# Projections and token sums as two 64-row products side by side, with PSUM in two-bank tiles

## The chip, the cores and the metric

The kernel runs on one core of one Trainium2 chip. Its time is the device time of one execution in microseconds (us); the figure to be predicted is the median of the runs of the changed kernel.

## What is computed

The reference runs four residual blocks over 2048 tokens of width 512, A, B, A, B, each on a layer norm of x. H = 32 heads of 16 columns.

```python
def _A_ref(x, wq, wk, wv, wo, beta):          # segments of 512 tokens, four of them
    ...
    for s in range(N):
        logits = jnp.einsum('bhqd,bhkd->bhqk', qs, ks) * scale + mask
        p = _softmax(logits, axis=-1)
        a_dot = jnp.einsum('bhqk,bhkd->bhqd', p, vs)
        pq = phi(qs)
        num = jnp.einsum('bhld,bhde->bhle', pq, M)
        den = jnp.einsum('bhld,bhd->bhl', pq, z)[..., None] + 1e-06
        o = g * (num / den) + (1.0 - g) * a_dot
        pk = phi(ks)
        M = M + jnp.einsum('bhld,bhle->bhde', pk, vs)
        z = z + jnp.einsum('bhld->bhd', pk)
    return o @ wo

def _B_ref(x, wqkv, w_phi, wo):
    ...
    phi_q = jnp.concatenate([_softmax(pq, axis=-1), _softmax(-pq, axis=-1)], axis=-1)
    phi_k = jnp.concatenate([_softmax(pk, axis=-1), _softmax(-pk, axis=-1)], axis=-1)
    kv = jnp.einsum('bhsf,bhsd->bhfd', phi_k, v)
    z = jnp.einsum('bhsf->bhf', phi_k)
    o = num / den                              # as above, with phi_q, kv and z
    return o @ wo

x = x + _A_ref(_layernorm(x), ...); x = x + _B_ref(_layernorm(x), ...)   # twice
```

The mask of A lets a query see the keys up to and including itself, inside its segment. All tensors are bf16; sums are kept in f32.

## The kernel before

x stays in SBUF as 16 tiles of 128 tokens (`X`). Everything is written as operations in a graph (`Graph.op`), each with the tiles it reads and writes. The order of all operations and the buffer of every tile are not decided when the kernel is built: they come from a table, `ORDER`, that was worked out beforehand and is unpacked in `Graph.place`. `Graph.emit` then walks through that order and puts a semaphore wait ahead of an operation wherever a dependency on another engine is not yet covered. Two operations of PE need none between them, since PE works in program order.

The stages, for each of the two layers:

- `ln` makes the layer norm of a token tile and transposes it into `xT`, mostly by a DMA transpose (`tr`), sometimes on PE through PSUM (`tpe`).
- `a_proj` makes, for one segment of four token tiles and each of four groups g of eight heads, K and Q with the group's columns on the partitions (`wproj`), and V with tokens on the partitions. Each is a sum over four blocks of 128 input columns, so four products of 128 rows and 512 columns into one PSUM bank. K and Q are copied to SBUF (`Kev`, `Qev`); K is also spread into masked copies (`Km`), and `phi` makes the feature maps. The segment's memory sums (`M`) are products over tokens, 136 columns wide.
- `a_att` makes, for a query tile i and each group, the transposed scores in 64-row products: half of the array works on heads from partitions 0 to 63, the other half on those from 64 to 127, and each writes a PSUM bank of its own. ACT takes the exponential, and the products with V (34 columns, 64 rows) accumulate over the keys in two banks `PV`. `a_mem` adds the memory's part. `out_proj` transposes the tile's output and multiplies it by the output weights, four products of 512 columns; the residual is added from PSUM, either by DVE or, where `RES_PE` says so, by a fifth product with the identity.
- `b_keys` makes K and V of block B per token tile (`vproj`), the exponentials, and the token sums (`KV`), 136 columns for each of eight slots, three slots to a bank, added up by `kv_add`.
- `b_query` makes Q of block B (`wproj`, two groups into one two-bank tile), exponentials, the denominators (`Zq`), the products with the sums (`N`) and the output projection.

A product of 64 rows names its half of the array by a tile position; in this text, products of 128 rows and products of 64 rows are two modes of the array. Scores, the products with V, `NM` and `N` have 64 rows, all other products have 128.

PSUM has eight banks. The kernel holds them in two pools:

```python
dbl = [self.es.enter_context(nc.psum_tensor(f"D{i}", [128, 1024], F32)) for i in range(2)]
sgl = [self.es.enter_context(nc.psum_tensor(f"G{i}", [128, 512], F32)) for i in range(4)]
```

`pD`, two tiles of two banks, takes scores, `N`, `NM` and the queries of B. `pG`, four tiles of one bank, takes the projections, transposes and sums (class `gen`), the accumulators (`pv`, two at a time) and the denominators (`nz`). In the profile they appear as D and G.

Of the kernel before, what the change touches and what calls it, by code (L numbers as in the profile page):

```python
# [16 lines left out]
D = 512  # L17
H = 32
# [65 lines left out]
class Op:  # L84
    __slots__ = ("id", "ch", "deps", "succ", "tiles", "opens", "nd", "prio", "eng", "start", "end", "kind", "lat",
                 "label", "seq", "idx", "need", "waits", "tick", "sem", "ndma", "vc", "__dict__")
# [3 lines left out]
class Graph:  # L90
# [39 lines left out]
    def op(self, ch, reads=(), writes=(), opens=(), kind="c", lat=None, label="", ndma=0, port=False, kb=0, rows=128):  # L130
        o = Op()
        o.id = len(self.ops)
        o.ch = ch
        o.deps = set()
        o.succ = []
        o.tiles = []
        o.opens = list(opens)
        o.kind = kind
        o.lat = lat
        o.label = label  # L140
        o.ndma = ndma
        o.need = False
        o.port = port
        o.kb = kb
        o.rows = rows
        o.vc = None
        for r in reads:
            self._touch(o, r, False)
        for w in writes:
            self._touch(o, w, True)  # L150
        o.deps.discard(o)
        self.ops.append(o)
        return o
# [35 lines left out]
    def emit(self):  # L189
# [25 lines left out]
        for o in order:  # L215
# [17 lines left out]
            cand = [d for d in deps if not (d.kind == "c" and d.eng == "pe" and e == "pe") and not covers(kn, d)]  # L233
# [63 lines left out]
class Kernel:  # L297
# [30 lines left out]

    def act(self, out_ap, in_ap, func, n, reads, writes, opens=(), scale=1.0, psum=True, label=""):
        dur = n / 1.2 + (51 if psum else 93)  # L330
        return self.g.op({"act": (dur, lambda e: e.activation(out_ap(), in_ap(), func, scale=scale))},  # L331
                         reads, writes, opens, label=label)
# [18 lines left out]
    def tpe(self, out_ap, src, reads, writes, opens=(), label="", ev=None):  # L351

        ps = self.T(self.pG, "gen")
# [22 lines left out]
    def alloc(self):  # L376
# [44 lines left out]
        dbl = [self.es.enter_context(nc.psum_tensor(f"D{i}", [128, 1024], F32)) for i in range(2)]  # L421
        sgl = [self.es.enter_context(nc.psum_tensor(f"G{i}", [128, 512], F32)) for i in range(4)]
        self.pD = Pool("pD", dbl, psum=True)
        self.pG = Pool("pG", sgl, psum=True)
        self.pG.caps = CAPG
        self.pG.fifo = ("pv",)
        self.pools = [self.pK, self.pX, self.pQ, self.pV, self.pW, self.pE, self.p1, self.p2, self.pT, self.pS, self.pD, self.pG]
# [94 lines left out]
    def fold_weights(self):  # L522
# [12 lines left out]
        for k in ("k", "q"):  # L535
# [7 lines left out]
            for dt in range(4):  # L543
                ps = self.T(self.pG, "gen")
# [40 lines left out]
    def wproj(self, ps, col, W, wres, g, xT, opens=(), label=""):  # L585
        self.mm(lambda: [(ps.t[:, col:col + 512], W[:, dt, g * 128:(g + 1) * 128], xT.t[:, dt, :], dt == 0, dt == 3) for dt in range(4)],
                [512] * 4, [xT[i] for i in range(4)] + wres, [ps[col]], opens=opens, label=label)

    def vproj(self, ps, W, wres, tt, xT, opens=(), label=""):
        self.mm(lambda: [(ps.t[:, 0:512], xT.t[:, dt, tt * 128:(tt + 1) * 128], W[:, dt, :], dt == 0, dt == 3) for dt in range(4)],  # L590
                [512] * 4, [xT[tt]] + wres, [ps[0]], opens=opens, label=label)

    def phi(self, ps, dst, src=None):
# [3 lines left out]
        self.act(lambda: e_.t[:], lambda: ps.t[:, 0:512], ACT.Exp, 512, [ps[0]], [e_], label="phexp")  # L597
        if src is None:
            self.g.op({"dve": (602, lambda e: e.tensor_scalar(dst.t[:], ps.t[:, 0:512], 0.0, None, op0=ALU.max)),
                       "act": (478, lambda e: e.activation(dst.t[:], ps.t[:, 0:512], ACT.Relu))}, [ps[0]], [dst], label="phmax")  # L600
        else:
            v(lambda e: e.tensor_scalar(dst.t[:], src.t[:], 0.0, None, op0=ALU.max), 202, [src], [dst], label="phmax", port=True)
# [23 lines left out]
    def a_proj(self, L, s):  # L626
# [7 lines left out]
        for g in range(NG):  # L634
            ps = self.T(self.pG, "gen")
# [3 lines left out]
            KM = self.T(self.pQ, "KM")  # L639
            pk = self.T(self.p1, "phiKT") if s < 3 else None  # L640
            self.wproj(ps, 0, self.WA["k"], [R("WA", "k", g // 2)], g, xT, opens=[KT] + ([pk] if pk else []), label="K")
# [16 lines left out]
            ps = self.T(self.pG, "gen")  # L658
            QT = self.T(self.pK, "QT")
            PQ = self.T(self.p1, "phiQ") if s >= 1 else None  # L660
            self.wproj(ps, 0, self.WA["q"], [R("WA", "q", g // 2)], g, xT, opens=[QT] + ([PQ] if PQ else []), label="Q")
            self.evac(lambda QT=QT: QT.t[:], lambda ps=ps: ps.t[:, 0:512], 512, [ps[0]], [QT], label="Qev")
            st["QT"].append(QT)
            if PQ:
                self.phi(ps, PQ, QT)
                st["PhQ"].append(PQ)
        for tt in range(4):
            ps = self.T(self.pG, "gen")
            self.mm(lambda tt=tt, ps=ps: [(ps.t[:, 0:512], xT.t[:, dt, tt * 128:(tt + 1) * 128],
                                           self.WA["v"][:, dt, :].rearrange("p (k a e) -> p a k e", k=8, a=2), dt == 0, dt == 3) for dt in range(4)],  # L670
                    [512] * 4, [xT[tt]] + [R("WAv", i) for i in range(4)], [ps[0]], opens=[VT], label="V")
            self.evac(lambda tt=tt: VT.t[:, tt, :, 0:16], lambda ps=ps: ps.t[:, 0:512].rearrange("p (h d) -> p h d", h=H),
                      512, [ps[0]], [VT[tt]], label="Vev")
# [7 lines left out]
        if s < 3:  # L681
            for hp in range(2):
                ps = self.T(self.pG, "gen")
                gs = (hp * 2, hp * 2 + 1)
                self.mm(lambda gs=gs, ps=ps: [
                    (ps.t[:, (g % 2) * 136:(g % 2 + 1) * 136].rearrange("p (k a e) -> p a k e", k=2, a=2), st["PhK"][g].t[:, tt * 128:(tt + 1) * 128],
                     VT.t[:, tt].rearrange("p (a k r) c -> p a k (r c)", a=2, r=2)[:, :, 2 * g:2 * g + 2, :], tt == 0, tt == 3) for g in gs for tt in range(4)],
                        [136] * 8, [st["PhK"][g] for g in gs] + [VT[i] for i in range(4)], [ps[0]], label="M")
                pv = lambda ps=ps: ps.t[:, 0:272].rearrange("p (g h c) -> p g h c", g=2, h=8)
# [8 lines left out]

    def pvitem(self, PV, c, P, V, st, sp):

        a = PV.t[:, c:c + 17]
# [4 lines left out]
    def a_mem(self, L, s, i):  # L706
# [5 lines left out]
        if i == 0:  # L712
            st["mem"] = []
            Rm = st["rm"] = self.T(self.pS, "Rm")
            mc = self.T(self.pG, "nz")
            col = lambda q, g: mc.t[:, (q // 2) * 64:(q // 2) * 64 + 64].rearrange("p (a t g h) -> p a t g h", a=2, t=2, g=NG)[:, :, q % 2, g, :]
            self.mm(lambda: [(col(q, g), PQ[g].t[:, q * 128:(q + 1) * 128], self.MSb[mb][:, g, :, 16], True, True)
                             for q in range(4) for g in range(NG)], [8] * 16, list(PQ) + ms, [mc], opens=[Rm], label="NMd")
            self.g.op({"act": (158.0, lambda e: e.activation(Rm.t[:, 0:128], mc.t[:, 0:128], ACT.Ln, bias=self.eps6[:, 0:1]))},
# [12 lines left out]
    def a_att(self, L, s, i):  # L732
# [11 lines left out]
        PV = [self.T(self.pG, "pv") for _ in range(2)]  # L744
        for g in range(NG):
# [36 lines left out]
            def pvmm(PTs=PTs, g=g, hfs=(0, 1)):  # L782
                r = []
                for hf in hfs:
                    for p in range(2):
                        k = 4 * g + 2 * hf + p
                        for j in range(i + 1):
                            for x in range(2):
                                for ab in range(2):
# [6 lines left out]
                                    r.append(self.pvitem(PV[ab], 18 * k, P, V, j == 0 and x == 0, j == i and x == 1))  # L796
                return r
            vs = [VS[(z, hf)] for z in range(i * VSP // 4 + 1) for hf in range(2)]
            for hfs in ((0,), (1,)) if i in SPLIT else ((0, 1),):
                self.mm(lambda pvmm=pvmm, hfs=hfs: pvmm(hfs=hfs), [], PTs + [PTs[i][0], PTs[i][1]] + [VT[j] for j in range(i + 1)] + vs,  # L800
                        [PV[0][(g, hfs[0])], PV[1][(g, hfs[0])]], label="PV", rows=64, dur=4 * len(hfs) * (i + 1) * 25.5)
        for ab in range(2):
            pvv = lambda ab=ab: PV[ab].t[:, 0:288].rearrange("p (h c) -> p h c", c=18)
            rd = lambda ab=ab: rden().rearrange("p (k a r) -> p k a r", a=2, r=2)[:, :, ab, :]
            v(lambda e, pvv=pvv, rd=rd: self.recip(e, rd(), pvv()[:, :, 16].rearrange("p (k r) -> p k r", r=2)), self.dur_recip(16),
              [PV[ab][(g, h)] for g in range(NG) for h in (range(2) if i in SPLIT else range(1))], [Rt[ab]], label="rden")
# [3 lines left out]
              [PV[ab][(g, h)] for g in range(NG) for h in (range(2) if i in SPLIT else range(1))] + [Rt[ab]], [o[ab]], label="pvn")  # L810
# [5 lines left out]
        self.out_proj(t, o, [o[0], o[1]], self.WA["o"], [R("WA", "o")], pe=("a", L, t) in PE_T)  # L816

    def out_proj(self, t, o, ores, W, wres, store=False, res_pe=False, pe=False, pair=None):
        R = self.R
        oT = self.T(self.p1, "oT")  # L820
        if pair is not None:
            tp = self.T(self.pG, "gen")
# [9 lines left out]
        elif pe:  # L832
# [3 lines left out]
        ps = self.T(self.pG, "gen")  # L836
        if res_pe:
            self.mm(lambda: [(ps.t[:, 0:512], self.ident[:], self.X[:, t, :], True, False)] +
                    [(ps.t[:, 0:512], oT.t[:, dt * 128:(dt + 1) * 128], W[:, dt, :], False, dt == 3) for dt in range(4)],
                    [512] * 5, [oT, R("X", t), R("ident")] + wres, [ps[0]], label="Wo")  # L840
            self.evac(lambda: self.X[:, t, :], lambda: ps.t[:, 0:512], 512, [ps[0]], [R("X", t)], label="res")
        else:
            self.mm(lambda: [(ps.t[:, 0:512], oT.t[:, dt * 128:(dt + 1) * 128], W[:, dt, :], dt == 0, dt == 3) for dt in range(4)],
                    [512] * 4, [oT] + wres, [ps[0]], label="Wo")
# [322 lines left out]
```

## Time and profile before

| | before |
|---|---|
| median of 3 runs | 508.94 us (506.62 to 509.52) |
| the profiled execution | 507.85 us, of which the span of the profile is 506.1 |
| PE matmul | 461.6 us busy (91%), 10514 recorded |
| PE weight load | 291.1 us (58%), 10610 |
| DVE | 437.6 us (86%), 1088 instructions |
| ACT | 439.1 us (87%), 612 |
| granted PE clock, mean over the span | 0.99 |
| DMA | 30.25 MB, 60 GB/s on the mean |

The profile is one execution, recorded by the hardware. "Busy" is the time in which an engine had an instruction under way; matmuls overlap in the array, so a matmul's own duration (380 ns for 512 columns) is longer than the time between the starts of two of them. A row such as `D<-pK,pQ 64*128 64x128` is a product into a tile of the pool D, with 64 rows, 128 output partitions and 128 columns. Some matmul records are missing from the trace; all weight loads are there.

### The profile page before, as it was taken

The numbers are of one execution on the slowest core, as the hardware profiler recorded it, in microseconds if no ns is written. First come the engines' busy times: TensorE is split into PE (matmuls) and PEld (weight loads), VectorE is DVE, ScalarE is ACT, GpSimd is POOL, SyncE is SP. The second block draws the span as 40 slices with busy tenths as digits, with TensorE's granted clock in tenths as the row PEclk, the third lists the DMA queues.
The fourth block names the chain that finished last, engine by engine and source line by source line (L and its number), as shares of the span: only waits on it lengthen the run. The fifth ranks groups of instructions, "written<-read, shape, count | busy, mean of one in ns | idle before, by whom it ended". The sixth has DMA issues, their size and how long they took to land.

```text
span 506.1 us, 23397 instructions
## 1 busy us (share of the span) xinstructions
PE 461.6 (91%) x10514; PEld 291.1 (58%) x10610; DVE 437.6 (86%) x1088; ACT 439.1 (87%) x612; POOL 60.1 (12%) x144
## 2 busy tenths in 40 slices
PE   8899899999888979999999898988998898899896
PEld 4356656555666666555545665566566656565543
DVE  5999969998887978989999888988988788899795
ACT  3899899999899979589999899998998898858993
POOL 3602201100010011101310120110001101010000
PEclk9999989999999999999999999999999999999799
DMA  8943744321213031000235636221221313200165
GB/s 240 230 103 65 105 63 72 42 59 30 52 31 54 4 49 30 12 3 12 33 70 80 76 67 76 54 50 21 55 46 25 45 24 49 31 13 0 37 123 157
DMA packets 89444, 30.25 MB, mean 60 GB/s; under 512 B 76000, under 2 KB 89344, under 8 KB 89344
## 3 DMA queue, kind: packets, MB, share of 16 engines
q1 hardware_dynamic: 88992, 28.46, 30.8%
q8 instruction: 83, 1.36, 1.1%
q10 hardware_dynamic: 288, 0.26, 0.2%
q14 instruction: 17, 0.14, 0.1%
q0 software_dynamic: 64, 0.02, 0.1%
HBM read 6.32 MB, written 2.10 MB: 17 GB/s over the span
## 4 chain that ended last, share of the span: by engine, by line
PE 64%; ACT 13%; DVE 11%; issue 6%; DMA 3%; POOL 2%; POOLq 0%
PE G L325 42%; PE D L325 21%; ACT p L331 9%; ACT pE L331 2%; DVE pQ L644 2%; DMA p<-p 2%; DVE stats L554 2%; DMA beta_sb<-in_A_beta_dram 1%; DVE X L845 1%; POOL rstd L564 1%; PE G L827 1%; DVE p L575 1%; ACT pS L331 1%; DVE p L340 0%; DVE p L985 0%
## 5 line engine op out<-in xcount | busy, mean ns | idle before, releaser
L331 ACT ACTIVATE p<-D 128x1024 bf16<-128x1024 f32 x256 | 256.4, 1039 | 16.2 <-PE D L325 14.9
L325 PE MATMUL D<-pK,pQ 64*128 64x128 bf16 (+1 forms) x2560 | 114.1, 212 | 7.1 <-issue 2.7
L331 ACT ACTIVATE pE<-D 128x768 bf16<-128x768 f32 x128 | 103.0, 828 | 18.7 <-PE D L325 18.2
L325 PEld LDWEIGHTS D<-pK,pQ 64*128 64x128 bf16 x2560 | 71.6, 94 | 60.0 <-issue 20.1
L325 PE MATMUL G<-pV,p 64*128 64x34 bf16 (+1 forms) x1632 | 79.4, 178 | 5.0 <-issue 4.3
L331 ACT ACTIVATE p<-G 128x512 bf16<-128x512 f32 x112 | 67.9, 624 | 13.7 <-PE G L325 11.8
L325 PEld LDWEIGHTS G<-pV,p 64*128 64x128 bf16 (+1 forms) x1632 | 71.4, 93 | 10.0 <-issue 5.8
L325 PE MATMUL G<-pW,pE 64*128 64x34 bf16 x1024 | 71.6, 175 | 5.5 <-issue 5.5
L325 PE MATMUL G<-pV,pE 64*128 64x34 bf16 x1024 | 73.9, 175 | 0.5 <-issue 0.5
L325 PE MATMUL G<-pW,p 64*128 64x34 bf16 x1536 | 70.7, 176 | 1.8 <-issue 1.8
L325 PEld LDWEIGHTS G<-pW,p 64*128 64x128 bf16 x1536 | 64.6, 93 | 2.5 <-issue 2.0
L562 POOL TENSOR_SCALAR rstd<-mv 128x1 f32<-128x1 f32 x60 | 15.6, 265 | 382.9 <-DVE mv L555 382.8
L325 PEld LDWEIGHTS G<-pV,pE 64*128 64x128 bf16 x1024 | 53.4, 93 | 2.5 <-issue 2.4
L325 PEld LDWEIGHTS G<-pW,pE 64*128 64x128 bf16 x1024 | 50.9, 92 | 6.1 <-issue 6.1
L644 DVE TENSOR_SCALAR pQ<-p,m 128x512 bf16<-128x512 bf16 x128 | 43.9, 364 | 0.2
L554 DVE BATCH_NORM_STATS2 stats<-X 128x6 f32<-128x512 bf16 x64 | 43.1, 684 | 0.8 <-DMA X<-in_A_x_dram 0.2
L906 DVE TENSOR_REDUCE pS<-p 128x32 f32<-128x512 bf16 x64 | 42.0, 671 | 1.4 <-ACT p L331 1.4
L845 DVE TENSOR_TENSOR X<-X,G 128x512 bf16<-128x512 bf16 x48 | 32.6, 682 | 10.6 <-PE G L325 10.3
L888 DVE TENSOR_TENSOR pT<-G,pT 128x1024 bf16<-128x1024 f32 x30 | 36.0, 1212 | 2.7 <-PE G L325 2.2
L564 POOL TENSOR_TENSOR rstd<-rstd,mhalf 128x1 f32<-128x1 f32 x60 | 36.2, 610 | 3.2
L325 PE MATMUL D<-tri,two 64*128 64x256 bf16 x256 | 35.4, 272 | 0.8 <-issue 0.8
L325 PE MATMUL G<-WB_o,p 128*128 128x512 bf16 x120 | 31.2, 385 | 1.9 <-issue 1.0
(117 smaller groups left out, 806.1 us busy)
## 6 DMA issues: line engine op xcount, KB each, us to landing
pW<-pV SPq DMA_DIRECT2D x16, 136.0 KB, 2.7
out_dram<-X SPq DMA_DIRECT2D x16, 128.0 KB, 1.9
X<-in_A_x_dram SPq DMA_DIRECT2D x3, 512.0 KB, 7.4
pX<-in_B_wqkv_dram SPq DMA_DIRECT2D x3, 512.0 KB, 7.0
p<-p SPq DMA_TRANSPOSE x76, 2.5
pX<-p SPq DMA_TRANSPOSE x54, 2.8
WA_v<-in_A_wv_dram SPq DMA_DIRECT2D x1, 512.0 KB, 6.0
WB_o<-in_B_wo_dram SPq DMA_DIRECT2D x8, 64.0 KB, 3.3
```

Source lines behind the costliest of these rows:

```text
L325: ins = e.matmul(out_ap, lhsT, rhs, start=st, stop=sp, tile_position=(basep(lhsT), basep(out_ap)))
L331: return self.g.op({"act": (dur, lambda e: e.activation(out_ap(), in_ap(), func, scale=scale))}, reads, writes, opens, label=label)
L554: v(lambda e: e.bn_stats(self.stats[:, t, :], self.X[:, t, :]), 602, [R("X", t)], [R("st", t)], label="bn")
L562: v(lambda e: e.tensor_scalar(rs, self.mv[:, t, 1:2], LN_EPS, None, op0=ALU.add), 170, [R("mv", t)], [R("rstd", t)], eng="pool", label="rstd")
L564: v(lambda e: e.tensor_tensor(rs, rs, self.mhalf[:], ALU.pow), 540, [R("rstd", t), R("mhalf")], [R("rstd", t)], eng="pool", label="rstd")
L575: v(lambda e: e.tensor_scalar(xn.t[:], self.X[:, t, :], self.mv[:, t, 0:1], self.rstd[:, t:t + 1], op0=ALU.subtract, op1=ALU.mult), 300, [ ...
L644: fn = lambda e, KM=KM, KT=KT, sl=sl: e.tensor_scalar(KM.t[:, :, sl % 2, :, 64 * (sl // 2):64 * (sl // 2) + 64], KT.t[:].rearrange("p (j h ...
L827: ins = e.matmul(tp.t[:, k * 128:(k + 1) * 128], pair.t[:, (k // 2) * 512 + sgn * 256 + (k % 2) * 128:(k // 2) * 512 + sgn * 256 + (k % 2) ...
L845: self.v(lambda e: e.tensor_tensor(self.X[:, t, :], self.X[:, t, :], ps.t[:, 0:512], ALU.add), 602, [R("X", t), ps[0]], [R("X", t)], label ...
L888: v(lambda e: e.tensor_tensor(dst(), ps.t[:, None, 0:512].to_broadcast([128, 2, 512]).rearrange("p s (g d h) -> p s g d h", g=NG, h=8), rz ...
L906: fn = lambda e, sgn=sgn, E=E, Z=Z: e.tensor_reduce(Z.t[:, sgn * 32:(sgn + 1) * 32], E.t[:, sgn * 512:(sgn + 1) * 512].rearrange("p (h d) ...
```

## The change

Every projection and token sum becomes a pair. Two outputs, in the two banks of one PSUM tile, are made at the same time: in the first half of the operation rows 0 to 63 of all input blocks work for the first output and rows 64 to 127 for the second; in the second half the banks are exchanged. The two halves are two operations of the graph, so the order may put other work between them, and the second waits by semaphore until the first has ended (`hard`), which is the first case in this kernel of PE waiting for itself.

```diff
+    def pair(self, items, cols, reads, writes, opens=(), label=""):
+        def half(k):
+            def fn(e):
+                ab = items()
+                lists = (ab[k], ab[1 - k])
+                ins = None
+                for i in range(max(len(x) for x in lists)):
+                    for hf in range(2):
+                        if i < len(lists[hf]):
+                            out_ap, lhsT, rhs = lists[hf][i]
+                            ins = e.matmul(out_ap, lhsT[64 * hf:64 * hf + 64], rhs[64 * hf:64 * hf + 64], start=k == 0 and i == 0, stop=k == 1 and i == len(lists[hf]) - 1,
+                                           tile_position=(64 * hf, 0))
+                return ins
+            return fn
+        dur = sum(max(c / 2.4 + 3.0, 25.5) for c in cols)
+        o1 = self.g.op({"pe": (dur, half(0))}, reads, writes, opens, label=label, rows=64)
+        return self.g.op({"pe": (dur, half(1))}, reads, writes, label=label + "2", rows=64, hard=o1)
...
-            cand = [d for d in deps if not (d.kind == "c" and d.eng == "pe" and e == "pe") and not covers(kn, d)]
+            cand = [d for d in deps if (d is o.hard or not (d.kind == "c" and d.eng == "pe" and e == "pe")) and not covers(kn, d)]
...
-        dbl = [self.es.enter_context(nc.psum_tensor(f"D{i}", [128, 1024], F32)) for i in range(2)]
-        sgl = [self.es.enter_context(nc.psum_tensor(f"G{i}", [128, 512], F32)) for i in range(4)]
+        dbl = [self.es.enter_context(nc.psum_tensor(f"D{i}", [128, 1024], F32)) for i in range(4)]
...
+    def wproj(self, ps, Ws, wres, gs, xT, opens=(), label=""):
+        self.pair(lambda: [[(ps.t[:, k * 512:k * 512 + 512], W[:, dt, g * 128:(g + 1) * 128], xT.t[:, dt, :]) for dt in range(4)]
+                           for k, (W, g) in enumerate(zip(Ws, gs))],
+                  [512] * 4, [xT[i] for i in range(4)] + wres, [ps[0], ps[512]], opens=opens, label=label)
...
-            self.wproj(ps, 0, self.WA["k"], [R("WA", "k", g // 2)], g, xT, opens=[KT] + ([pk] if pk else []), label="K")
+            self.wproj(ps, (self.WA["k"], self.WA["q"]), [R("WA", "k", g // 2), R("WA", "q", g // 2)], (g, g), xT,
+                       opens=[KT, QT] + ([pk] if pk else []) + ([PQ] if PQ else []), label="KQ")
```

What is paired with what: K with Q of one group; V of two token tiles; the memory sums of two groups; K, and V, of block B for two token tiles; the queries of B for two groups; the output projections of two token tiles, so that an even tile's projection waits for the odd tile's output. Where only one token tile is at hand (the last two tiles of each block, listed in `SOLO`, and the two tiles left over where block B takes the last segment as three tiles and one) the tile's 512 columns are halved, 256 to each bank (`tproj` with one tile). The sums of B now come four slots to a two-bank tile, so `kv_add` runs twice a part and no longer three times. The small products of `NMd` and `Zq` become 64-row products, one half of the array for each bank. `RES_PE` names the pairs (2, 3), (6, 7), (10, 11) and (14, 15) in place of the odd tiles, as many as before.

All PSUM tiles come from one pool of four two-bank tiles, also those that use one bank (`tpe`, the folded weights, `otp`); `PV` is one two-bank tile. The table `ORDER` is another one: order, engines and buffers of all operations are worked out anew. The transposes on PE, the folding of weights, the `otp` products and the warm-up keep their 128 rows.

## The prediction

> **What bounds the kernel now.** I read the page from the top: span 506.1 us, and three engines that are all busy.
>
> ```profile
> PE 461.6 (91%) x10514; PEld 291.1 (58%) x10610; DVE 437.6 (86%) x1088; ACT 439.1 (87%) x612; POOL 60.1 (12%) x144
> ...
> q8 instruction: 83, 1.36, 1.1%
> ...
> PE 64%; ACT 13%; DVE 11%; issue 6%; DMA 3%; POOL 2%; POOLq 0%
> ```
>
> The chain that ended last (third line) lies on PE for 64%. Busy shares flatter ACT and DVE, because consecutive instructions overlap at their ends, so next I read the timelines, where starts can be subtracted.
>
> ```profile
> 55.79 1.94 ACT L331 ACTIVATE p<-D 128x1024 bf16<-128x1024 f32 x2
> 57.62 0.60 ACT L331 ACTIVATE p<-G 128x512 bf16<-128x512 f32 x1
> 58.09 0.83 ACT L331 ACTIVATE pE<-D 128x768 bf16<-128x768 f32 x1
> ```
>
> Two 1024-wide exponentials take 57.62 - 55.79 = 1.83 us, 0.915 each, though one is listed with 1.039. At such pitches (0.70 for 768, 0.48 for 512) ACT's work adds up to about 417 us, and DVE's, in the same way, to about 400.
>
> PE's own timeline shows what its time consists of:
>
> ```profile
> 102.79 1.04 PE L325 MATMUL G<-WB_k,pX 128*128 128x512 bf16 x4
> 103.76 0.62 PE L325 MATMUL D<-pK,pQ 64*128 64x128 bf16 x16
> 104.32 1.04 PE L325 MATMUL G<-WB_v,pX 128*128 128x512 bf16 x4
> 105.19 1.03 PE L325 MATMUL G<-pX,WA_q 128*128 128x512 bf16 x4
> ```
>
> Four 512-column products followed by four more take 105.19 - 104.32 = 0.87 us; followed by 64-row score products they take 103.76 - 102.79 = 0.97. A change between 128-row and 64-row work costs about 0.1 us. Over all matmul starts of the trace: a 512-column product is followed after 215 ns by its like, after 311 by a 64-row one; a pair of 64x128 products after 53 ns by the next pair, after 148 by a 128-row product; a 64x256 pair after 107 or 202. That is 95 ns per change, either way, and there are 342 changes.
>
> A second cost shows inside one run of P·V products, where no operand is waited for:
>
> ```profile
> 100.05 0.20 PE L325 MATMUL G<-pW,p 64*128 64x34 bf16 x2
> 100.90 0.17 PE L325 MATMUL G<-pV,p 64*128 64x34 bf16 x1 [0.65 <-issue]
> ```
>
> PE issued 10610 weight loads, 10610 matmuls and 134 semaphore waits; 83 packets of the instruction queue (1.36 MB) make 256 of these per packet. Counted through, 20 of the 83 block boundaries have such a stop, 19.5 us in all, 1.64 us the longest, and no block took under 3.03 us. Work of under about 3.3 us per 256 instructions makes PE wait for its code.
>
> PE's account is thus: streams 423.3 us (columns at the pitches above; 59 ns for 136 columns, 25 for 34 and fewer; halves counted as pairs), mode changes 342 x 0.095 = 32.5, code 19.5, together 475.3. The other 30.8 us of the span are start, end, waits for ACT, DVE and DMA, and two stretches (3.4 and 6.8 us) with granted clock 0.5. PE needs 475 where ACT needs 417 and DVE 400: PE is the bound.
>
> **The change, part by part.**
>
> Streams. 1040 products of 128 rows x 512 columns become 972 steps of two 64-row products of 512 columns and 136 steps of 256, and 352 of 136 columns replace 352. A step does what one product did. The trace has no 64x512 pair; its 64x128, 64x256 and 64x34 pairs start 2 to 4 ns apart and pass at 53, 107 and 25 ns, the pitch of one product of these widths. Bounds for a 512-column step: 213 ns (columns at that rate) and 430 (no overlap at all); nearest is the 256 row, so 215. Total 423.4, change +0.1. The small products `NMd` and `Zq` also become pairs at the 25 ns step: nothing.
>
> [...]
>
> Mode changes. In the new order of PE only the transposes, the folding products, the `otp` products and the warm-up have 128 rows: 49 changes. 293 x 0.095 = -27.8 us, all on the engine that sets the end.
>
> Code. PE's instructions grow by 1880 matmuls with their loads, and 162 waits on itself appear; 98 blocks instead of 83. Taking each block's streams and changes and 3.3 us as the least per block, the old order gives 18.5 us of stops (19.5 seen), the new one 23.1: +4.6. With 3.0 or 3.5 us the difference is +2.0 or +6.2.
>
> Bank exchange. Before the second half of a pair PE waits for the first half's last matmul. That one takes 380 ns (512 columns), and a matmul that waits for another engine starts some 55 ns behind the release; without the wait it would come after 215. So 220 ns of other work must stand between. What is queued behind the wait is everything on PE, and ACT and DVE behind that. In the new order 151 of 162 waits have at least 204 ns of their own cover (mostly eight score products, 223 ns), the rest miss up to 219: +1.7 us. With no cover anywhere it would be 162 x 0.22 = 36 us.
>
> ACT, DVE, SP. ACT loses 7 evacuations (-3.4 us), DVE gains about ten casts and saves on fewer `KVacc` (+2.6). SP issues as many DMAs, 192; the residual of an even tile now comes with that of the odd one, as its output projection waits for the second transpose. ACT at 414 and DVE at 402 stay below PE. These costs hide behind PE.
>
> PSUM. Six buffers (two of two banks, four of one) become four of two. Held times in the trace: a score tile 1.73 us, an accumulator pair 8.0, K 4.4, Q 3.8, V 2.9 us. I price this through the waits: if nothing is added, 0; upward it is the first rival.
>
> Sum: 423.4 + 4.7 + 24.1 + 1.7 = 453.9 us of PE need, 21.4 less. With the other 30.8 us unchanged, the span is 484.7. Those do not stay fixed: some 20 of them are waits for other engines, and PE's lead over ACT shrinks from 58 to 40 us. Growing inversely to the lead they add 10; a roomier order could also take a few off. I take +5: span 490. The profiled execution took 507.85 for its span of 506.1, and the median of the runs is 508.94, 2.8 above that span. So 492 us.
>
> **Rivals.**
>
> First, slower: too few PSUM buffers. While a tile's accumulator holds one buffer and two projections or transposes hold two, one is left for scores. Then ACT cannot exponentiate one while PE fills the next: it stands for 51 ns of release, 165 for three steps and 258 from the last product's start to ACT's, 0.47 us for each score tile. For it: buffers were held 74% (pairs) and 70% (singles) of the span. With the held times above, 1.7 us more for each of the 168 paired tiles (second product, cover, second evacuation) against its two singles' mean, I come to 1760 buffer-us, 90% of four at 490. Against it: a shared buffer serves whoever comes, and held times contain slack. Of 384 score tiles, 35 in this state eat the gain left after the +5, and over 41 make it slower by 0.5%. A fifth of them, 77, give 490 + 36, some 520 to 530 on the runs' scale. [...]
>
> Second, most of the gain is lost because ACT or DVE binds in stages. Between 40 and 60 us ACT is busy 19.89 of 20 us, DVE 19.17. If in half of the span nothing follows PE, 10 to 11 of the 21 us remain missing on top of the +5: 503 to 511. Against it: at pitches ACT has 17% of slack.
>
> Third, the change does not do what it says: loads or halves do not overlap at 512 columns. A load of 95 ns exposed per step is 1040 x 0.095 = 99 us, so 590. The 53 and 107 ns rows speak against it.
>
> **How the numbers follow.** A measurement here tells 0.5% (2.5 us) from no change. Forecast 0.64, own range 482 to 503, with 0.05 of it below that; first rival 0.20, second 0.13 (about half of it still faster by over 0.5%, below 506.4, half within), third 0.03. Faster 0.64 + 0.07 = 0.71, same 0.06, slower 0.20 + 0.03 = 0.23. The range 482 to 515 leaves out 0.05 below, 0.12 of the first rival and the third: 2 in 10.
>
> **What would show it.** Right: rows of 64x512 with starts 215 ns apart per pair; about 49 mode changes; 98 packets on q8 and 20 to 27 us of stops at block boundaries; PE idle little before the second halves; ACT at about 413 us of pitch in a shorter span. Wrong: PE waiting for ACT before score products, or ACT for PE on D, by more than the 33 us that `p<-D` and `pE<-D` have now (first rival); long loads between the halves (third); ACT without idle slices while PE waits (second).

## The result, and the profile after

The changed kernel takes 493.06 us (median of 4 runs, 492.54 to 495.05), the kernel before 509.23 beside it (506.62 to 511.52): a ratio of 0.969 with a 95% interval of 0.964 to 0.975. Run again later, it took 494.25 us (ratio 0.968, 0.964 to 0.973). The profiled execution took 492.6 us for a span of 490.9; 492 and 490 were forecast. That the total came out so close hides two terms that did not, as the account below shows.

The page of the changed kernel, the lines that answer to the first three shown of before:

```profile
PE 460.2 (94%) x12490; PEld 309.1 (63%) x12490; DVE 436.1 (89%) x1087; ACT 433.9 (88%) x605; POOL 59.6 (12%) x144
...
q8 instruction: 98, 1.61, 1.4%
...
PE 59%; ACT 25%; DVE 8%; issue 3%; DMA 3%; SPq 1%; POOL 0%; POOLq 0%; DVEq 0%
```

PE issues 1880 matmuls more in 15 us less and is still the engine on most of the chain. ACT's part of the chain has grown from 13 to 25%.

ACT's timeline (start, duration): two full score tiles take 101.07 - 99.13 = 1.94 us (1.83 in the rows shown of before), then come the diagonal ones.

```profile
99.13 2.05 ACT L351 ACTIVATE p<-D 128x1024 bf16<-128x1024 f32 x2
101.07 1.51 ACT L351 ACTIVATE pE<-D 128x768 bf16<-128x768 f32 x2
```

PE's timeline around one pair, K with Q of a group:

```profile
104.47 0.39 PE L341 MATMUL D<-pX,WA_k 64*128 64x512 bf16 x1
104.47 0.39 PE L341 MATMUL D<-pX,WA_q 64*128 64x512 bf16 x1
104.70 0.38 PE L341 MATMUL D<-pX,WA_k 64*128 64x512 bf16 x1
104.70 0.38 PE L341 MATMUL D<-pX,WA_q 64*128 64x512 bf16 x1
...
105.13 0.38 PE L341 MATMUL D<-pX,WA_k 64*128 64x512 bf16 x1
105.13 0.38 PE L341 MATMUL D<-pX,WA_q 64*128 64x512 bf16 x1
105.34 0.39 PE L326 MATMUL D<-pK,pQ 64*128 64x128 bf16 x8
105.57 0.39 PE L341 MATMUL D<-pX,WA_q 64*128 64x512 bf16 x1
105.58 0.39 PE L341 MATMUL D<-pX,WA_k 64*128 64x512 bf16 x1
```

K and Q start together and the next step follows after 212 to 216 ns (the first here after 0.23 us), which is the pitch of one 128-row product (215 ns before). The score products follow the last step after 0.21 us, where the kernel before paid 0.31. They are the cover of the exchange: the second half starts 0.44 us after the last step of the first (105.13 to 105.57), with K and Q in each other's place, and PE has lost nothing. (L326 is `mm`, L341 is `pair`, L351 and L359 are ACT's; in the kernels edited below these lines stand a little higher or lower.)

The waits of the changed kernel (who waited for whom: us in total, times, longest):

```profile
PEld D L326 <- ACT p L351: 16.7, 45, 1.4
PEld D L341 <- issue: 11.8, 23, 1.9
ACT p L351 <- PE D L326: 11.6, 21, 1.5
ACT p L351 <- PE D L341: 10.3, 12, 2.6
...
PEld D L341 <- PE D L341: 3.0, 7, 0.6
```

The last line is PE waiting for itself: 7 times, 3.0 us in all. Waits of score products for ACT have fallen. The weight loads of score products alone, before and after (count | busy us, mean ns | idle us before them and what ended it):

```profile
L325 PEld LDWEIGHTS D<-pK,pQ 64*128 64x128 bf16 x2560 | 71.6, 94 | 60.0 <-issue 20.1 <-ACT p L331 17.4 <-ACT pE L331 11.2
L326 PEld LDWEIGHTS D<-pK,pQ 64*128 64x128 bf16 x2560 | 80.7, 94 | 43.4 <-ACT p L351 10.9 <-ACT pE L351 5.0 <-DVE p L756 1.4
```

They waited 28.6 us for ACT (17.4 and 11.2), and now wait 15.9 (10.9 and 5.0).

Set against the prediction's account, in us of span:

| | before | predicted | after |
|---|---|---|---|
| streams | 423.3 | 423.4 | 423.4 |
| mode changes | 32.5 | 4.7 | 4.7 |
| stops at block boundaries | 19.5 | 24.1 | 13.2 |
| bank exchange | 0 | 1.7 | 3.0 |
| the rest | 30.8 | 35.8 | 46.6 |
| span | 506.1 | 489.7 | 490.9 |

Below, "standing time" is the sum of all delays of a matmul's start behind the one before it, beyond the pitch and 95 ns for a mode change. It is 51.0 us in the changed kernel; what remains of the span outside streams, changes and standing time (start, end, a stretch of 10.2 us from 454.8 at a granted clock of 0.50) is 11.8 us.

### The profile page after: what moved, and what is told of

The parts are those of the page before. It is cut to its first block, busy times and chain, and to the rows that moved or that the text cites. A ratio compares the mean times of both kernels' runs of the same rounds, so it can differ in the third digit from the quotient of the medians.

```text
span 490.9 us, 27235 instructions
## 1 busy us (share of the span) xinstructions
PE 460.2 (94%) x12490; PEld 309.1 (63%) x12490; DVE 436.1 (89%) x1087; ACT 433.9 (88%) x605; POOL 59.6 (12%) x144
## 4 chain that ended last, share of the span: by engine, by line
PE 59%; ACT 25%; DVE 8%; issue 3%; DMA 3%; SPq 1%; POOL 0%; POOLq 0%; DVEq 0%
PE D L341 36%; PE D L326 21%; ACT p L351 16%; ACT pE L351 6%; DMA WA_q<-in_A_wq_dram 2%; DVE pQ L672 1%; ACT pS L351 1%; DVE p L756 1%; DVE pS L925 1%; PE D L854 1%; DVE pK L360 1%; ACT pV L359 1%; DVE p L591 1%; ACT p L359 1%; DVE p L360 1%
## 5 line engine op out<-in xcount | busy, mean ns | idle before, releaser
L351 ACT ACTIVATE p<-D 128x1024 bf16<-128x1024 f32 (+1 forms) x368 | 312.1, 913 | 25.2 <-PE D L326 11.6
L326 PE MATMUL D<-pK,pQ 64*128 64x128 bf16 (+1 forms) x2560 | 115.5, 211 | 4.3 <-ACT p L351 1.4
L326 PEld LDWEIGHTS D<-pK,pQ 64*128 64x128 bf16 x2560 | 80.7, 94 | 43.4 <-ACT p L351 10.9
L351 ACT ACTIVATE pE<-D 128x768 bf16<-128x768 f32 x128 | 102.0, 835 | 4.7 <-PE D L326 3.6
L326 PE MATMUL D<-pV,p 64*128 64x34 bf16 x1536 | 73.4, 176 | 3.9 <-issue 2.9
L326 PE MATMUL D<-pV,pE 64*128 64x34 bf16 x1024 | 75.2, 175 | 0.5 <-ACT pE L351 0.2
L326 PE MATMUL D<-pW,pE 64*128 64x34 bf16 x1024 | 73.0, 175 | 0.1
L326 PE MATMUL D<-pW,p 64*128 64x34 bf16 x1536 | 71.7, 176 | 1.0 <-issue 0.9
L326 PEld LDWEIGHTS D<-pV,p 64*128 64x128 bf16 x1536 | 66.8, 93 | 7.1 <-issue 2.4
L326 PEld LDWEIGHTS D<-pW,p 64*128 64x128 bf16 x1536 | 65.8, 93 | 3.9 <-issue 1.4
L341 PE MATMUL D<-pX,WA_k 64*128 64x512 bf16 x256 | 65.2, 376 | 2.1 <-DMA WA_q<-in_A_wq_dram 1.4
L341 PE MATMUL D<-pX,WA_q 64*128 64x512 bf16 x256 | 65.3, 377 | 0.6 <-issue 0.4
L326 PEld LDWEIGHTS D<-pV,pE 64*128 64x128 bf16 x1024 | 54.8, 93 | 3.1 <-issue 1.5
L326 PEld LDWEIGHTS D<-pW,pE 64*128 64x128 bf16 x1024 | 51.2, 93 | 0.9 <-issue 0.3
L341 PE MATMUL D<-WA_o,p 64*128 64x512 bf16 (+1 forms) x288 | 33.8, 353 | 2.3 <-issue 1.9
L326 PE MATMUL D<-tri,two 64*128 64x256 bf16 x256 | 35.2, 270 | 0.0
```

Of the source, the lines that this page charges most:

```text
L326: ins = e.matmul(out_ap, lhsT, rhs, start=st, stop=sp, tile_position=(basep(lhsT), basep(out_ap)))
L341: ins = e.matmul(out_ap, lhsT[64 * hf:64 * hf + 64], rhs[64 * hf:64 * hf + 64], start=k == 0 and i == 0, stop=k == 1 and i == len(lists[hf ...
```

## The experiments

**Undoing the row mode.** In the changed kernel's order and buffers, each operation of a pair makes one whole output with 128-row products; then the same for K, Q and the queries of B alone.

```diff
-                lists = (ab[k], ab[1 - k])
-                ...
-                            ins = e.matmul(out_ap, lhsT[64 * hf:64 * hf + 64], rhs[64 * hf:64 * hf + 64], ..., tile_position=(64 * hf, 0))
+                w = items()[k]
+                for i, (out_ap, lhsT, rhs) in enumerate(w):
+                    ins = e.matmul(out_ap, lhsT, rhs, start=i == 0, stop=i == len(w) - 1, tile_position=(0, 0))
...
-        return self.g.op(..., label=label + "2", rows=64, hard=o1)
+        return self.g.op(..., label=label + "2", rows=128)
```

> The changed kernel with its order, buffers and two-bank tiles, but each operation of a pair makes one whole output with products of 128 rows in its own bank: no halves, no bank exchange, no wait of PE on itself. The order now has 464 changes between 128-row and 64-row work where the changed kernel has 49, and about 86 blocks of 256 instructions where it has 98. My theory (the gain is the mode changes): 415 x 0.095 = +39 us, less 3 for the exchanges that go and 0 to 10 for waits that fall into the longer PE time: 519 to 529 us. Rival (the gain comes from the new order and the PSUM pool, not from the row mode): 488 to 497. Rows will show 128x512 products 311 ns ahead of a 64-row one.

Measured: 518.19 us (ratio to before 1.016, 1.012 to 1.020), 25 us above the changed kernel and just under the forecast. PE's timeline shows the changes back:

```profile
93.46 1.04 PE L337 MATMUL D<-WB_k,pX 128*128 128x512 bf16 x4
94.33 1.03 PE L337 MATMUL D<-pX,WA_k 128*128 128x512 bf16 x4
95.29 0.40 PE L326 MATMUL D<-pK,pQ 64*128 64x128 bf16 x8
95.62 1.04 PE L337 MATMUL D<-pX,WA_q 128*128 128x512 bf16 x4
```

Four products followed by four more take 0.87 us (93.46 to 94.33), followed by scores 0.96; eight score products take 0.33 us (95.29 to 95.62) where the changed kernel's take 0.23.

> The same for K with Q and the queries of block B alone (48 of the 168 pairs): 199 changes, 150 more than the changed kernel. My theory: 150 x 0.095 = +14 us, less up to 1 for the exchanges that go and up to 4 absorbed by waits: 502 to 507 us, and the step per change the same as in the run with all pairs undone. Rival (order and PSUM): 490 to 496.

Measured: 508.96 us (0.998, 0.995 to 1.002), 15 to 16 us above the changed kernel for 150 changes, and 2 us over the forecast. What follows: in this order the pairs are worth the mode changes that they save, less what waits take back. The large run gave 25 us and not 36, because standing time fell from 51.0 to 36.6: with a slower PE, other engines are waited for less (some 3 us of the fall lie at block boundaries).

Order and PSUM pool together bring little: with all pairs undone the kernel has 122 changes more than the kernel before, worth 11.6 us, and is 8.5 us slower. That little is a sum of two opposite parts, though. In the trace of this run the stops at block boundaries come to some 10 us where the kernel before has 19.5, so its other waits are some 8 us longer than those of the kernel before.

**The exchange without cover.** First with the first half moved to just ahead of the second, then in this same order without the exchange.

```diff
+        sec = {o.hard: o for o in order if o.hard}
+        order = [x for o in order if o not in sec for x in ((o.hard, o) if o.hard else (o,))]
```

> The changed kernel with the first half of every pair moved in PE's order to just ahead of its second half, so that nothing covers the bank exchange. My theory: 168 waits x 0.22 us = 37 us, of which 3 are paid already, so +34: 520 to 528 us, and at each exchange the first product of the second half starts some 435 ns after the last of the first half. Rival (PE waits for ACT and for its code anyway, and an exchange falls into that): 493 to 503.

```diff
-                lists = (ab[k], ab[1 - k])
+                lists = (ab[0], ab[1])
...
-        return self.g.op(..., label=label + "2", rows=64, hard=o1)
+        o2 = self.g.op(..., label=label + "2", rows=64)
+        o2.mate = o1      # place() moves by mate instead of hard
```

> The order of the run before (first half just ahead of the second), but the second half keeps the banks and does not wait; the sums are then not the reference's, the work of every engine is the same in kind and amount. It separates the wait from the moved order. My theory: the moved order alone costs little (first halves start later, so a buffer is held shorter): 488 to 496 us, 30 to 37 us below the run with the wait. If the order itself matters (scores ahead of first halves move nothing, evacuations come at the same time), up to 500.

Measured: 563.73 us (1.106, 1.101 to 1.111) with the exchange and 531.80 (1.043, 1.038 to 1.047) without. The difference, 31.9 us or 0.19 us for each of 168 waits, is as expected. (There is one wait for each of the 168 pairs; in the changed kernel's own order other waits cover six of them, which leaves the prediction's 162.) PE's timeline with the exchange, and the line of the waits:

```profile
123.34 0.38 PE L343 MATMUL D<-pX,WA_k 64*128 64x512 bf16 x1
123.35 0.83 PE L343 MATMUL D<-pX,WA_q 64*128 64x512 bf16 x2
123.79 0.39 PE L343 MATMUL D<-pX,WA_k 64*128 64x512 bf16 x1
```

```profile
PEld D L343 <- PE D L343: 80.9, 168, 1.0
```

The step across the exchange takes 0.45 us (123.34 to 123.79) in place of 0.215; the 80.9 us count each wait from the weight load on, so they hold the step that would have passed anyway.

Both times themselves were missed, by some 36 us: the moved order alone costs 38. The waits of the run without exchange:

```profile
PEld D L328 <- ACT p L355: 37.3, 59, 1.4
PE D L328 <- ACT p L355: 27.3, 48, 1.2
PEld D L328 <- ACT pE L355: 22.8, 39, 1.0
ACT p L355 <- PE D L328: 21.6, 30, 2.1
ACT p L355 <- PE D L343: 17.4, 20, 2.4
```

Score products that had stood between the halves now come 0.86 us earlier, wait for ACT to free their buffer, and hold up both halves, which stand behind them and could have run; after that ACT waits for PE, which has 1.72 us of projection ahead of the next scores. Standing time rises from 51.0 to 91.7 us. So the products between the halves do more than cover the exchange: they hand ACT its work in smaller steps. That the buffer is what they wait for is read from these lines; no run tried it by itself.

The exchange taken away in the order of the changed kernel, beside the changed kernel itself:

> The changed kernel in its own order, without the exchange: the second half keeps the banks of the first and does not wait, so that the sums are not the reference's. My theory (the order covers the exchanges; what is left uncovered was seen as 3.0 us): 2 to 4 us below the changed kernel, 488 to 492 us. Rival (in this order too the waits hold PE and all behind it much more than their own rows say): 10 us or more below.

> The changed kernel unaltered, beside the others of this call: 492 to 495 us, 3.1% under the kernel before. It is what the other runs of this call are compared with.

Measured: 492.70 us (0.966, 0.962 to 0.971) against 494.25 (0.968, 0.964 to 0.973). The 1.6 us lie inside the intervals; with the 3.0 us of the waits they rule out the rival's 10. Those 3.0 us, too, count from the weight load on: by the starts of the products the waits delay PE by some 1.6 us.

**Is ACT the bound?** Exponentials of 168 score tiles over half of their columns, in both kernels.

```diff
-                    self.act(lambda PT=PT: PT.t[:], lambda S=S: S.t[:], ACT.Exp, 1024, [S], ...)
+                    n = 1024 if (L, s) == (0, 0) else 512
+                    self.act(lambda PT=PT, n=n: PT.t[:, 0:n], lambda S=S, n=n: S.t[:, 0:n], ACT.Exp, n, [S], ...)
```

> The changed kernel with the exponentials of 168 full score tiles over half of their columns (the others keep stale values, so the output is not the reference's): ACT has 168 x 0.435 = 73 us less to do, PE's work is the same. My theory: of the some 50 us in which PE stands, those that wait for ACT go, but block boundaries stop it more, since a wait no longer gives the code time to arrive: 470 to 482 us, with 20 to 27 us of stops at block boundaries where the changed kernel has 13. If ACT has become an equal bound (second rival of the prediction): below 470. If ACT does not matter: 489 or more.

> The kernel before with the exponentials of 168 full score tiles over half of their columns, as was done to the changed kernel, where it took off 2.7 us (the output is not the reference's). My theory (PE is the bound in both; what PE waits for on ACT is mostly the way from a tile's last score to its first product with V): 2 to 5 us less, 504 to 507. If ACT had been less near to the bound here than in the changed kernel: no change.

Measured: 491.58 us (0.965, 0.960 to 0.971) for the changed kernel, 2.7 less than unaltered; 507.21 (0.996, 0.993 to 0.999) for the kernel before, 1.6 less. I had expected 11 to 24 us in the first, and that theory fell. The windows from 240 to 260 and 260 to 280 us, of the changed kernel and then of the light one (busy us of PE, PEld, DVE, ACT, POOL; granted clock):

```profile
240.00:260.00 20.00, 19.55 (x300) 10.48 (x302) 19.62 (x62) 19.84 (x34) 3.92 (x8) 1.00 0.20 41
260.00:280.00 20.00, 19.39 (x514) 14.00 (x510) 19.42 (x53) 20.00 (x26) 3.16 (x8) 1.00 0.48 86
```

```profile
240.00:260.00 20.00, 19.42 (x299) 10.26 (x298) 19.62 (x60) 18.18 (x35) 3.92 (x8) 1.00 0.28 45
260.00:280.00 20.00, 19.85 (x518) 14.01 (x514) 19.89 (x53) 15.80 (x27) 3.20 (x8) 1.00 0.61 87
```

ACT has 4.2 us of air in the second window, and PE gets through no more than before (518 matmuls, 514 without the air). DVE is busy for 19.4 to 19.9 of 20 us in all four windows, so that DVE holds PE here is not excluded by this run. PE's standing time is 51.5 us, as before; by what the late product had waited for, ACT's share falls from 21 to 16 us, DVE's rises from 6 to 10 and the stops at block boundaries from 13.2 to 16.6 (the trace of the second run of the unaltered kernel has some 2 us more of them than that of the first). ACT's amount of work is no bound in either kernel.

**Moving the block boundaries.** Products of 8 columns in the warm-up push all later instructions on; the work after them is untouched.

```diff
+                for _ in range(18 if n == 64 else 0):     # 44 in the kernel before
+                    for r0 in (0, 64):
+                        ins = e.matmul(D.t[:, r0 * 8:r0 * 8 + 8], self.onesb[r0:r0 + 64, :], self.onesb[r0:r0 + 64, 0:8], start=True, stop=True, tile_position=(r0, 0))
```

> The changed kernel with 36 more products of 8 columns (64 rows, 0.45 us in all) in PE's warm-up, while it waits for the first inputs: all that follows is the same, but every instruction stands 72 places further from the block boundaries of its code. The prediction's rule (least 3.3 us for 256 instructions, each block's streams and mode changes against it) gives 29.2 us of stops in place of 21.2, the worst of all places. If stops for code are a cost on the path: 4 to 8 us slower, 497 to 502. If waits for other engines cover them, or if the blocks do not matter: 492 to 495.

> The kernel before with 88 such products (1.1 us, of which up to 1 may show at the start), so that every instruction stands 176 places further: the rule gives 10.2 us of stops in place of 19.8, the least of all places. If stops for code are a cost on the path: 4 to 9 us faster than before, 500 to 505. If not: 509 to 511.

Measured: 501.75 us (0.985, 0.981 to 0.989) for the changed kernel, 7.5 to 8.7 slower than unaltered; 498.19 (0.979, 0.975 to 0.982) for the kernel before, 10.6 faster. Stops at block boundaries, by the rule at the recorded positions and as seen in the traces:

| | rule | seen |
|---|---|---|
| before | 19.8 | 19.5 |
| before, 176 places on | 10.0 | 10.9 |
| after | 21.2 | 13.2 |
| after, 72 places on | 29.2 | 21.4 |

One such stop, on PE's timeline of the shifted changed kernel, in the middle of P·V products:

```profile
185.49 0.19 PE L326 MATMUL D<-pW,pE 64*128 64x34 bf16 x2
187.62 0.17 PE L326 MATMUL D<-pV,pE 64*128 64x34 bf16 x1 [1.94 <-issue]
```

PE stands 2.1 us between two products that are 25 ns apart elsewhere, and the trace shows no operand that it waits for. Counted in instructions from PE's first weight load, nearly all stops of this kind stand at the same two neighbouring places of 256, in the changed kernel and in both shifted ones. In the changed kernel 25 stops of over 0.08 us are there, and 20 of them end 1.2 to 1.6 us after a packet of q8 has landed; in the kernel before, 17 of the 18 stops of over 0.3 us at products that wait for no operand do (1.3 to 1.6 us). So the stops are a cost on the path, and the rule gets the effect of a shift right to a microsecond in both kernels.

Could one use it? Over all 128 shifts of two places the rule gives the changed kernel between 19.8 and 29.2 us. It stands near the best already, so I let the rule choose four places inside for small shifts:

```diff
+FILL = ((17, 4), (230, 2), (285, 15), (288, 13))     # pairs of 8-column products ahead of these runs of score products
```

> The changed kernel with 34 pairs of 8-column products (0.9 us in all) at four places of PE's order, ahead of score products and into the same tile, which then overwrites them: 4, 2, 15 and 13 pairs, placed by the rule so that the block boundaries fall better (18.2 us of stops with the added products' own time counted in, in place of 21.2). If the rule is right to a microsecond or so: 2 to 4 us below the changed kernel, 489 to 492. If its differences are right only for large moves of all boundaries: 492 to 495.

Measured: 495.71 us (0.970, 0.965 to 0.975): no gain. The rule is good for moving all boundaries, not for gaining three microseconds.

**Going on with the change.** The transposes on PE, the folding and the `otp` products as 64-row pairs too.

```diff
-                ins = e.transpose(pb()[:, k * 128:(k + 1) * 128], src()[:, k * 128:(k + 1) * 128], self.ident[:])
+                for hf in range(2):
+                    r = slice(64 * hf, 64 * hf + 64)
+                    ins = e.matmul(ps.t[:, hf * 512 + k * 64:hf * 512 + k * 64 + 64], src()[r, k * 128:(k + 1) * 128], self.ident[r, r],
+                                   start=True, stop=True, tile_position=(64 * hf, 0))
```

> The changed kernel with its last 128-row work turned as well: the transposes on PE, the folding products and the products that transpose sums of two terms as 64-row products, one half of the array for each bank. 9 mode changes remain of 49; 26 PSUM tiles are then evacuated from two banks, transposes in f32 where they were bf16. My theory: 40 x 0.095 = 3.8 us less on PE, up to 2 of it lost to the longer evacuations and to waits: 489 to 492 us, 1 to 4 under the changed kernel. Rival (evacuation of a transpose is on the way at the start and the end of the kernel, where PE isn't the bound): no change, or up to 3 us slower.

Measured: 502.87 us (0.985, 0.980 to 0.990), 8.6 slower than the changed kernel, which neither theory nor rival had. The profiled execution is the slowest of the six (505.07). By the account streams and changes are 7.6 us less, but the added instructions move the boundaries to a worse place (19.1 us of stops seen, 13.2 in the changed kernel), and the first projection starts later, behind the load of `WA_q`, and at half clock (granted 0.5 from 13.3 to 16.7 us). The first two of K's products:

```profile
13.89 0.58 PE L341 MATMUL D<-pX,WA_k 64*128 64x512 bf16 x1 [2.22 <-DMA WA_q<-in_A_wq_dram]
...
14.27 0.63 PE L341 MATMUL D<-pX,WA_k 64*128 64x512 bf16 x1
```

A step takes 0.4 us here, until 16.8 us; the changed kernel starts at 11.95 after 1.39 us of idling, at full clock. At 30 us the run is 3.9 us behind. Standing time away from block boundaries is 51 us in place of 38; beyond those 3.9, what of it comes from the new evacuations stays open, and so does whether the late load belongs to the edit. No version that does the whole computation beat the changed kernel.

## Why the prediction was right, point by point

- **Streams.** +0.1 us, 215 ns a step: shown, 212 to 216 ns. The weight loads of both halves (for `pX,WA_k` 92 to 96 ns, median 94) add nothing to these steps. No run shows the 95 ns of exposed load a step that the third rival counts: it is out.
- **Mode changes.** -27.8 us: price and count shown. 49 changes are left at the same price (a 64x512 step is followed by a 128-row transpose after 308 ns, 95 more than by its like), and putting 150 or 415 changes back cost 15 and 25 us.
- **Bank exchange.** +1.7 us against 3.0 seen in 7 waits (some 1.6 by the starts of the products), and 0.19 us for each wait with no cover. The bound of 36 us for no cover anywhere is right for the wait itself (31.9 us), and less than half of what such an order costs.
- **Code.** This step failed in its size and sign: 24.1 us were forecast, 4.6 more than before, and 13.2 are seen, 6.3 less. The smaller part, 3.2 of the 10.9, was the count of instructions, taken from the order alone: at the recorded positions the rule gives +1.4. The main part is that the rule takes a block's work without its waits: in the changed kernel 8 us of it do not show, in both positions tried. That waits inside the block give the code time to come is argued. The trace agrees with it block by block: of some 18 us of stops that the rule gives and the trace lacks, some 15 are matched by waits inside the same blocks (and some 5 us are seen that the rule does not give). With ACT lightened the stops rose by 3.4 us only, not much more than two traces of one kernel differ.
- **The rest.** +5 forecast, +15.8 measured: the step is "growing inversely to the lead", which gave +10, of which +5 was taken. By the account of the shifted kernel before, whose records are complete, 11.5 us lie at start, end and half clock, so the kernel before stood some 19 us in waits other than for code (30.8 - 11.5), and the changed kernel 35 without the exchanges. The picture behind the step, that ACT's amount of work takes over as PE's falls, is refuted by the two light runs. What is left is the way from one engine to the next and back; such waits shift to DVE and to the code when ACT is quicker. Two readings narrow the 16 us down. With all pairs undone, waits other than for code are some 27 us already, so about half of the growth came with the new order and buffers, and half with the shorter PE work. And by what the late product had waited for, waits that ACT ended are some 9 us in the shifted kernel before, 16 with the pairs undone and 20 to 21 in the changed kernel. So most of the growth is waiting that ACT ends, though its amount of work is not the reason. No run took these waits away by themselves.
- **The sum.** The errors of code (-10.9) and the rest (+10.8) cancel, and belong together in part: a stop that a wait hides is booked under the wait. The forecast of their sum with the exchange, 61.6, met 62.8. That the span came out within 1 us of 490 is in good part luck: nothing in the working ties the two errors to each other.
- **First rival, PSUM.** Did not decide: the four tiles were held 86% of the span (90% estimated), a score tile 1.73 us as before, and waits for ACT's release fell. But what it describes shows in the moved order without the exchange: there the waits of score products' loads for ACT come to 47.1 us (26.4 for `p`, 20.7 for `pE`) in 75 waits, 0.63 each, where the estimate was 0.47. The pool is enough in the order that the changed kernel has.
- **Second rival, ACT or DVE binding.** ACT is out by the light runs; DVE, busy for nearly all of the windows shown, was not tried alone and stays open.

What the prediction did not see is how much of the two kernels' distance is where their code happens to be cut. The kernel before stands near its worst place (19.8 us by the rule, of 10.0 to 20.0 over all shifts), the changed one near its best (21.2 of 19.8 to 29.2). At its best place the kernel before takes 498.2 us (with 1.1 us of idle products in it), 4 to 5 more than the changed one as it is; at its worst the changed one takes 501.8, 7 less than the kernel before as it is. Of the 16 us some 4 to 7 do not hang on that.

## What to carry to other kernels

Subtract starts in PE's timeline to price a change between row modes (0.095 us here), count the changes in the order that will really run, and expect other waits to take back a good part: here changes that count 36 us were worth 25. Where a product has to wait for PE's own result, put the other engine's next work between the halves: here it hid 0.19 us a time, and it kept that engine fed, which was worth as much again (38 us beside 31.9). Before a few per cent are credited to an edit, shift both kernels' code with idle products: 72 and 176 places of 256 alone moved these two by 8 and 10 us.

## What the runs showed of the hardware that was not expected

- The place of a program in its blocks of 256 PE instructions is worth 2%: 88 idle matmuls of 8 columns, 1.1 us of work, made the kernel before 10.6 us faster, and 36 of them made the changed kernel some 8 us slower. The longest stop seen is 2.1 us.
- Near the start of a run, after 2.2 us without work, the first 2.9 us of products ran at about half rate (0.4 us a step in place of 0.215, granted clock 0.5); after 1.4 us at the start of the changed kernel they did not, nor after 1.98 us of idling up to 22.6 us in the kernel before (granted clock 1.0 in both). Each is one instance.
